# Seven products instead of eight for the last of the first MLP's second matmuls, and five smaller moves with it

## The chip, the cores and the metric

The kernel runs on one core of a Trainium2 chip. The metric is device time of one execution in microseconds (us). Engines are named as the profile names them: PE is TensorE's matrix multiply, PEld its weight load, DVE is VectorE, ACT is ScalarE, SP is the SyncE queue on which the DMA transfers are issued.

## What is computed

Linear attention with a decay for each head, and then two MLPs, one behind the other, on 3072 tokens of width 512 with a hidden width of 2048, all in float32:

```
state = gamma * state + einsum('bhd,bhe->bhde', k[t], v[t])
y[t]  = scale * einsum('bhd,bhde->bhe', q[t], state)
x = y.reshape(3072, 512)
h = x @ w_in;   g = h / (1 + exp(-1.702 * h));              x = g @ w_out
h = x @ w_in2;  g = max(h, 0) + alpha * min(h, 0);  out = g @ w_out2
```

The weights arrive as 64-bit words and are turned into float32 on the chip. An fp32 product is made of three: each operand is split into a high part that the fast matmul format holds exactly and a low rest (names ending in hi/lo, gh/gl, wh/wl, th/tl), and hi*hi, lo*hi and hi*lo are summed in PSUM.

## The kernel before

The tokens are six blocks of 512; each layer is worked off block by block. The program has three stretches.

**The plain part.** `steps` is a list of 32 steps (LEAD = 5 of block 0, all 16 of block 1, the other 11 of block 0). A step is one 128-wide slice of the hidden width: `mlp_h` (L531) makes 12 matmuls of 512 columns, the gate follows on ACT, `g_split` (L523) makes gh on ACT (L525) and gl on DVE (L526), and one step later `mlp_y` (L547) makes 12 matmuls into four PSUM banks (L558). Between the steps stand jobs, in numbered half-step slots: attention of a chunk of 128 tokens (`att_scores`, `att_out`, `att_x`), the conversion of weights, their stores to DRAM, and the sums of W_in slices (`conv_sums`, `conv_split`, slots in SUMS_IN). `base` is slot 64, the end of the plain part.

**The streamed pairs.** The other blocks of layer 1 and all of layer 2 come in five pairs (PAIRS, idx 0 to 4) of two token blocks. Their x @ w_in is made by seven products of 2 x 2 blocks instead of eight (the Strassen-Winograd scheme): a unit (`h_unit`) is one of the seven products for a quarter of a slice pair, 6 matmuls of 512 columns (L660) with one 256 KB weight piece `hw`, loaded in a ring that runs 6 units ahead. Eight quads of seven units make a pair. The partial results are joined on ACT (copies, L672) and DVE (adds, L675). Chunks 16 to 23 of the attention lie between the first 30 units or so.

The second matmul, g @ w_out, follows 36 units behind (YLAG). For idx 1 to 4 it has seven products too (`strassen_y`): a chunk is 6 matmuls (L758) with one 256 KB piece `yw`; it wants differences t1 to t4 of the gated blocks (L702), a split of each, and joins of the results (`y_out`, L771 on DVE, L781 on ACT). **For idx 0 it does not** (IDX_S = 1): it is made as in the plain part, by 12 matmuls a slice (`mlp_y`, in halves of 6), with hi and lo of W_out loaded again from DRAM (`woh`, `wol`, L644). In the second half of that, `slice_sums` and `conv_split` make the four sums of each W_out slice pair and store them (`wcout<-wb`), which idx 1 then uses.

**What sets the order.** Each engine runs its instructions in a fixed order. A framework makes that order from the order of the code, priorities (`tc.high_priority`) and its own estimates. The tiles live in 82 slots of SBUF (`take`, `give`), used again in the order in which they came free; a tile whose slot still has a store in flight must wait for that store. `give_stored` holds a slot back until `let_go` frees it a little later; the result tiles y of `mlp_out` and `y_out` use `give` at once. Loads of q, k, v and of the weight words go through a ring of five tiles (`issue`, `done`), in one order; the first chunks' q, k, v go through slots instead (`load_early`). SP's queue holds loads and stores in one order.

## Time and profile before

| | |
|---|---|
| three runs | 1059.97, 1061.17, 1063.59 us; median 1061.17 us |
| the profiled execution | 1063.32 us, its span 1061.5 us |
| PE busy, instructions | 1039.7 us (98%), 5980 |
| DVE busy, instructions | 847.8 us (80%), 1602 |
| ACT busy, instructions | 652.5 us (61%), 1344 |
| DMA | 292.07 MB, mean 275 GB/s |
| chain that ended last | PE 84%, DMA 7%, DVE 5%, ACT 3% |

The span is the time between the first and the last instruction; some 1.8 us of the execution lie around it. A matmul's record is longer than its share of the time, since the next begins before it has ended, so a busy PE need not be a PE at its peak. The windows view gives the busy time by stretches; in time, the plain part ends near 250 us, units alone run to 327 us, units and second matmuls by turns to 1006 us.

### The profile page before, as it was taken

The page shows a single profiled execution, that of the slowest core. Times are in us where ns is not written, and L with a number is a line of the kernel's source. Part 1 is how long each engine was busy: PE and PEld are TensorE (multiplying, and loading weights), DVE is VectorE, ACT ScalarE, POOL GpSimd, SP SyncE. Part 2 cuts the span into 40 slices and gives each one's busy share as a digit, 9 for nine tenths or more (in the row PEclk, how much of TensorE's full clock was granted, in tenths as well). Part 3 has the DMA queues.
Part 4 walks back from the last instruction along what each step waited for, and adds up shares of the span by engine and source line. Part 5 has one row for each costly group of instructions (what it writes and reads, how often), then busy time and mean ns, then how long its engine had stood idle before and what let it go on. Part 6 is the DMA issues. An engine that isn't in the chain of part 4 may idle for free.

```text
span 1061.5 us, 17729 instructions
## 1 busy us (share of the span) xinstructions
PE 1039.7 (98%) x5980; PEld 850.5 (80%) x5980; DVE 847.8 (80%) x1602; ACT 652.5 (61%) x1344; POOL 0.2 (0%) x4
## 2 busy tenths in 40 slices
PE   8999999999999999999999999989999999999998
PEld 5678877788878888888888878868888888888886
DVE  6999945584669877898899999999687897677792
ACT  6787744455566765556786586776555765546740
POOL 0000000000000000000000000000000000000000
PEclk9999999999999999999999999999999999999999
DMA  8679969779789999999999899978777775776571
GB/s 300 224 251 364 333 225 361 231 281 350 261 295 351 362 325 312 358 316 307 329 317 333 274 306 346 305 259 263 248 226 239 220 225 168 222 253 211 165 215 67
DMA packets 154139, 292.07 MB, mean 275 GB/s; under 512 B 16448, under 2 KB 33216, under 8 KB 154048
## 3 DMA queue, kind: packets, MB, share of 16 engines
q1 hardware_dynamic: 153760, 290.66, 81.1%
q8 instruction: 48, 0.79, 0.3%
q14 instruction: 43, 0.35, 0.1%
q10 hardware_dynamic: 288, 0.27, 0.1%
HBM read 214.32 MB, written 76.55 MB: 274 GB/s over the span
## 4 chain that ended last, share of the span: by engine, by line
PE 84%; DMA 7%; DVE 5%; ACT 3%; issue 1%; SPq 0%; DVEq 0%; ACTq 0%
PE py L758 26%; PE pa L660 18%; PE py L559 15%; PE pd L660 13%; PE ph L538 7%; DMA ld<-kv 2%; DMA wcin<-wb 2%; PE px L362 2%; PE sc L334 1%; DMA ld<-w 1%; DVE gl L526 1%; DVE a L345 1%; ACT v L327 1%; DMA early<-qk 1%; PE pu L362 0%
## 5 line engine op out<-in xcount | busy, mean ns | idle before, releaser
L660 PE MATMUL pa<-xo,hw 128*128 128x512 f32 x960 | 242.8, 390 | 1.9 <-ACT gw L517 1.6
L758 PE MATMUL py<-gh,yw 128*128 128x512 f32 x896 | 240.2, 389 | 1.0 <-DMA yw<-wcout 1.0
L660 PEld LDWEIGHTS pa<-xo,hw 128*128 128x128 f32 x960 | 179.7, 188 | 40.5 <-ACT gw L517 2.4
L758 PEld LDWEIGHTS py<-gh,yw 128*128 128x128 f32 x896 | 168.0, 188 | 36.8 <-DMA yw<-wcout 1.4
L660 PE MATMUL pd<-xo,hw 128*128 128x512 f32 x720 | 182.7, 390 | 0.0
L526 DVE TENSOR_TENSOR gl<-gw,gh 128x512 fp32r<-128x512 f32 x224 | 149.9, 685 | 38.9 <-ACT gh L525 34.5
L525 ACT CAST gh<-gw 128x512 fp32r<-128x512 f32 x224 | 135.8, 619 | 69.8 <-PE py L758 18.4
L660 PEld LDWEIGHTS pd<-xo,hw 128*128 128x128 f32 x720 | 134.8, 188 | 28.3
L758 PE MATMUL py<-gl,yw 128*128 128x512 f32 x448 | 138.2, 389 | 3.0 <-DVE gl L526 3.0
L758 PEld LDWEIGHTS py<-gl,yw 128*128 128x128 f32 x448 | 84.0, 188 | 20.7 <-DVE gl L526 3.4
L518 DVE SCALAR_TENSOR_TENSOR gw<-t,nalpha,gw 128x512 f32<-128x512 f32 x96 | 71.4, 746 | 18.6 <-ACT gw L517 18.3
L516 ACT ACTIVATE t<-gw 128x512 f32<-128x512 f32 x72 | 45.5, 632 | 49.9 <-DVE gw L675 49.3
L771 DVE TENSOR_TENSOR yc<-py,yc 128x512 f32<-128x512 f32 x79 | 50.7, 682 | 21.9 <-PE py L758 21.9
L212 ACT CAST wb<-s 128x256 fp32r<-128x256 f32 x128 | 48.0, 405 | 31.8 <-DVE s L279 16.5
L672 ACT COPY gw<-pa 128x512 f32<-128x512 f32 x80 | 46.5, 584 | 33.3 <-PE pa L660 32.4
L327 ACT ACTIVATE v<-ld,cst 128x64 f32<-128x64 f32 x168 | 44.5, 336 | 34.9 <-DMA ld<-kv 34.1
L675 DVE TENSOR_TENSOR gw<-pd,gw 128x512 f32<-128x512 f32 x80 | 54.6, 684 | 10.5 <-PE pd L660 10.5
L216 DVE TENSOR_TENSOR wb<-s,wb 128x256 fp32r<-128x256 f32 x128 | 50.2, 418 | 9.1 <-ACT wb L212 8.6
L538 PE MATMUL ph<-xhi,whi 128*128 128x512 f32 x128 | 52.3, 409 | 1.8 <-ACT xhi L420 1.1
L559 PE MATMUL py<-gh,whi 128*128 128x512 f32 x128 | 51.1, 399 | 0.7 <-ACT gh L525 0.7
L538 PE MATMUL ph<-xhi,wlo 128*128 128x512 f32 x128 | 51.3, 401 | 0.2 <-DVE wlo L242 0.2
L181 ACT ACTIVATE cvt<-ld 128x512 f32<-128x512 f32 x64 | 42.9, 673 | 12.4 <-DMA ld<-w 10.5
(100 smaller groups left out, 1616.7 us busy)
## 6 DMA issues: line engine op xcount, KB each, us to landing
hw<-wcin SPq DMA_DIRECT2D x280, 256.0 KB, 4.6
yw<-wcout SPq DMA_DIRECT2D x200, 256.0 KB, 3.8
ld<-w SPq DMA_DIRECT2D x64, 512.0 KB, 5.4
wcin<-wb SPq DMA_DIRECT2D x88, 256.0 KB, 4.8
wcout<-wb SPq DMA_DIRECT2D x88, 256.0 KB, 3.9
ld<-qk SPq DMA_DIRECT2D x21, 512.0 KB, 5.0
ld<-kv SPq DMA_DIRECT2D x21, 512.0 KB, 5.3
xl<-xsd SPq DMA_DIRECT2D x32, 256.0 KB, 5.3
```

Of the source, the lines that this page charges most:

```text
L212: nc.scalar.copy(out=w[:, 0:256], in_=src)
L216: nc.vector.tensor_tensor(out=w[:, 256:], in0=src, in1=w[:, 0:256].bitcast(F32), op=ALU.subtract)
L327: nc.scalar.activation(out=v[:, h, :], in_=vt[:, h * D:(h + 1) * D], func=AF.Copy, scale=decay_v[:, h:h + 1])
L518: nc.vector.scalar_tensor_tensor(out=g, in0=t, scalar=nalpha[:, ft:ft + 1], in1=g, op0=ALU.mult, op1=ALU.add)
L525: nc.scalar.copy(out=gh, in_=g)
L526: nc.vector.tensor_tensor(out=gl, in0=g, in1=gh.bitcast(F32), op=ALU.subtract)
L538: nc.tensor.matmul(out=ph, lhsT=w[:, k * P:(k + 1) * P], rhs=x[:, k, :], start=(n == 0), stop=(n == len(prods) - 1),)
L559: nc.tensor.matmul(out=py[e], lhsT=w, rhs=g, start=(begin and seen[e] == 1), stop=(end and seen[e] == 3))
L660: nc.tensor.matmul(out=ps, lhsT=w[:, 256 * part_ + k * P:256 * part_ + (k + 1) * P], rhs=x[2 * k + low], start=(n in (0, 1, 3) and m == 0) ...
L675: nc.vector.tensor_tensor(out=g, in0=ps, in1=g, op=ALU.add)
L758: nc.tensor.matmul(out=ps[e], lhsT=w[:, at:at + P], rhs=t, start=(fresh and seen[e] == 1), stop=(m == GQ - 1 and seen[e] == 3), skip_group ...
L771: add_ = lambda o, x: nc.vector.tensor_tensor(out=o, in0=ps, in1=x, op=ALU.add)
```

## The change

For idx 0 the second matmul becomes `strassen_y` as for the other pairs. The sums of the W_out slices are needed earlier for that and move into the plain part: slices 4 to 7 at slots 47 to 58, from hi and lo that are still on the chip, and slices 0 to 3 at slots 60 to 69, whose hi and lo are loaded again (`slice_load`). idx 0 therefore takes its slices in the order 4 to 7, 0 to 3, and the W_in sums are turned round in the same way. The q, k, v of chunks 16 to 23 come through slots, 2.5 slots ahead of their use. The products of v with the decay (L327) lose their priority. The differences t1 to t4 are each made a product earlier than they are used, where all of them stood with t2. The first six `yw` are loaded 12 units ahead, and result tiles y go through `give_stored`.

```diff
-IDX_S = 1
-QORD = [tuple(range(8)) if i != 1 else tuple(range(7, -1, -1)) for i in range(5)]
-WSTEPS = 6
-SUMS_IN = (37, 41, 45, 49, 53, 56, 59, 62)
+QORD = [(4, 5, 6, 7, 0, 1, 2, 3)] + [tuple(range(8))] * 4
+SUMS_IN = (53, 56, 59, 62, 37, 41, 45, 49)
+SUMS_OUT = (60, 63, 66, 69, 47, 51, 55, 58)
+LOADED = 4
...
+    def slice_load(i):
+        for f in (2 * i, 2 * i + 1):
+            assert ("out", 1, f) in stored
+            kept[f] = take("woh", dtype=F32R), take("wol", dtype=F32R)
+            for n in range(2):
+                nc.sync.dma_start(out=kept[f][n].bitcast(F32), in_=wo[f][n])
+
     def slice_sums(i):
         for f in (2 * i, 2 * i + 1):
+            ws = kept.pop(f, None)
+            hi, lo = ws or (w_hi["out", 1, f], w_lo["out", 1, f])
             raw["out", 1, f] = t = take("wsum")
-            hi, lo = wring[f]
...
-        with tc.high_priority(HG):
-            for h in range(H):
-                nc.scalar.activation(
...
+        for h in range(H):
+            nc.scalar.activation(
...
-            nc.sync.dma_start(out=dst, in_=y)
-            give(y)
-
-        return leave
+        nc.sync.dma_start(out=dst, in_=y)
+        give_stored(y)
...
             if which == "t2":
-                t2 = take("t2")
-                sub(g_of[b11], g_of[b12], g_of[b11])
-                sub(t2, g_of[b22], g_of[b11])
+                t2 = xt.pop(("y", b11))
+                ysplit[c] = g_split(t2, True)
                 sub(g_of[b21], g_of[b21], t2)
-                ysplit[c] = g_split(t2)
+                give(t2)
                 return
...
+            if which == "b11":
+                sub(g_of[b11], g_of[b12], g_of[b11])
+            if which == "b21":
+                t2 = xt["y", b11] = take("t2")
+                sub(t2, g_of[b22], g_of[b11])
+            if which == "t1":
+                sub(g_of[b12], g_of[b22], g_of[b12])
...
-        job(s_scores, att_scores, c, load=(("qk", c), ("kv", c)))
+        if c < 4 * per:
+            job(s_scores, att_scores, c, load=(("qk", c), ("kv", c)))
+        else:
+            job(s_scores - 2.5, load_early, c)
+            job(s_scores, att_scores, c)
...
+    for i in range(NQ):
+        if i < LOADED:
+            job(SUMS_OUT[i] - 2, slice_load, i)
+        job(SUMS_OUT[i], slice_sums, i)
+        job(SUMS_OUT[i] + 1, conv_split, "out", 1, i)
...
-    old = 4 * NF * IDX_S
     for u in range(len(units)):
         h_unit(u)
         past = u + 1 - YLAG
+        if past == -2 * YRING:
+            for c in range(YRING):
+                load_y(c)
         if past > 0:
-            y_turn(min(8 * past // NU, old) + max(0, past - old * NU // 8))
+            y_turn(past)
```

Three places show how the instructions move. The first is SP's queue near the end of the plain part, between the load of the sixth and of the seventh weight piece of the units (`hw`; `wcin` and `wcout` are the stored weights, `wb` a sum's two halves, `xl` the x of pair 0, `part` and `xsd` results). Before, its last rows:

```order
L249 DMA wcin_6_94<-wb 128x512
L644 DMA wol<-wo_121 128x512
L249 DMA wcin_7_95<-wb 128x512 x4
L644 DMA woh<-wo_122 128x512
L644 DMA wol<-wo_122 128x512
L644 DMA woh<-wo_123 128x512
...
L644 DMA wol<-wo_125 128x512
L608 DMA hw<-wcin_0_88 128x512
```

and now:

```order
L249 DMA wcout_0_104<-wb 128x512 x4
L294 DMA woh<-wo_122 128x512
L294 DMA wol<-wo_122 128x512
L597 DMA xsd_85<-y 128x512
L151 DMA ld<-w 128x1024
L597 DMA xsd_85<-y 128x512 x2
L151 DMA ld<-w 128x1024
L597 DMA xsd_85<-y 128x512
...
L169 DMA early<-kv 128x512 x2
L249 DMA wcin_3_91<-wb 128x512 x4
L613 DMA hw<-wcin_4_92 128x512
```

Stores of W_out sums, q, k, v of later chunks and words of layer 2's weights now stand ahead of the seventh piece. Counted in units of 256 KB, 65 transfers stood between the sixth and the seventh piece and 101 do now; up to the 21st piece it was 93 and is 147.

The second place is ACT's queue around steps 21 and 22, where block 1's results leave (`y`) and chunks 12 and 13 of the attention are worked on. Before:

```order
L513 ACTIVATE g<-ph 128x512
L525 CAST gh<-g 128x512
L327 ACTIVATE v<-ld,cst 128x64 x8
L581 COPY y<-py_1069 128x512
L581 COPY y<-py_1071 128x512
L212 CAST wb<-s_2334 128x256
L513 ACTIVATE g<-ph 128x512
L525 CAST gh<-g 128x512
L212 CAST wb<-s_2334 128x256
L327 ACTIVATE v<-ld,cst 128x64 x8
```

and now:

```order
L524 ACTIVATE g<-ph 128x512
L536 CAST gh<-g 128x512
L590 COPY y<-py_1069 128x512
L590 COPY y<-py_1071 128x512
L338 ACTIVATE v<-ld,cst 128x64 x16
L212 CAST wb<-s_2334 128x256 x2
L212 CAST wb<-s_2335 128x256
L524 ACTIVATE g<-ph 128x512
L536 CAST gh<-g 128x512
```

The eight products of v that chunk 12 needs stood behind the second gate (they are the later x8; chunk 13's stood first), and now stand ahead of it. The tiles g, gh, gl of that second gate and v of chunk 12 took the slots of the four y before; now they take others.

The third place is DVE's queue behind the last split of the plain part (`gl<-g,gh`), where the units begin (L675, now L666, joins their results; `a` is attention's mask). Before:

```order
L526 TENSOR_TENSOR gl<-g,gh 128x512
L470 TENSOR_TENSOR xo<-t_2824,xo 128x512
L575 TENSOR_TENSOR y<-py_2282,ld 128x512
...
L575 TENSOR_TENSOR y<-py_2285,ld 128x512
L675 TENSOR_TENSOR gw<-pd,gw 128x512 x2
L345 TENSOR_TENSOR a_3141<-sc_3131,cst 128x512
L345 TENSOR_TENSOR a_3143<-sc_3132,cst 128x512
L399 TENSOR_TENSOR t<-px,diag 128x256
```

and now:

```order
L584 TENSOR_TENSOR y<-py_2285,ld 128x512
L301 TENSOR_TENSOR wsum<-woh,wol 128x512
L279 TENSOR_TENSOR s_3201<-wsum 128x256
L216 TENSOR_TENSOR wb<-s_3201,wb 128x256
L666 TENSOR_TENSOR gw<-pd,gw 128x512 x2
L356 TENSOR_TENSOR a_3297<-sc_3287,cst 128x512
L356 TENSOR_TENSOR a_3299<-sc_3288,cst 128x512
L301 TENSOR_TENSOR wsum<-woh,wol 128x512
L279 TENSOR_TENSOR s_3200<-wsum 128x256
```

Sums of W_out slices stand between now, and the first of them waits for `woh` and `wol` from DRAM.

## Rows read from the trace of the kernel before

**Rows 1.** The chain that ended last, in order of time: start, length (us), what.

```profile
326.72 1.36 PE pa L660 x6
328.08 1.36 PE py L559 x6
...
1006.94 50.33 PE py L758 x222
```

**Rows 2.** Groups by line, whole run: busy us, mean ns | idle before.

```profile
L559 PE MATMUL py<-gh,woh 128*128 128x512 f32 x128 | 49.8, 389 | 0.0
```

**Rows 3.** Windows: length; busy us (count) of PE PEld DVE ACT POOL; clock, DMA share, GB/s.

```profile
60.00:140.00 80.00, 79.55 (x372) 65.50 (x363) 73.40 (x142) 59.89 (x117) 0.00 (x0) 1.00 0.95 329
...
325.00:405.00 80.00, 80.00 (x355) 66.26 (x354) 65.60 (x135) 50.74 (x105) 0.00 (x0) 1.00 0.97 347
405.00:490.00 85.00, 85.00 (x377) 70.41 (x376) 72.53 (x156) 48.35 (x102) 0.00 (x0) 1.00 0.97 331
...
540.00:600.00 60.00, 60.00 (x266) 49.73 (x265) 59.44 (x116) 44.37 (x90) 0.00 (x0) 1.00 0.92 305
600.00:660.00 60.00, 58.37 (x258) 48.00 (x257) 56.28 (x110) 40.26 (x81) 0.00 (x0) 1.00 0.93 321
660.00:720.00 60.00, 56.07 (x244) 45.30 (x243) 58.05 (x104) 46.37 (x92) 0.00 (x0) 1.00 0.87 292
```

**Rows 4.** Timeline of ACT, 172 to 184 us: start, length, what, [idle before].

```profile
179.49 0.60 ACT L513 ACTIVATE g<-ph 128x512 f32<-128x512 f32 x1 [4.34 <-DMA xsd<-y]
...
181.81 2.01 ACT L327 ACTIVATE v<-ld,cst 128x64 f32<-128x64 f32 x8
```

**Rows 5.** Timeline of PE, 181 to 183 us.

```profile
182.21 0.99 PE L362 MATMUL px<-v,ld 128*64 128x64 f32 x7 [1.64 <-ACT v L327]
```

**Rows 6.** Windows, columns as in rows 3.

```profile
183.40:190.20 6.80, 6.80 (x49) 5.26 (x48) 1.85 (x5) 1.03 (x4) 0.00 (x0) 0.50 0.83 278
```

**Rows 7.** Windows for the DMA rate, columns as in rows 3.

```profile
160.00:180.00 20.00, 20.00 (x209) 15.87 (x207) 10.95 (x24) 7.98 (x23) 0.00 (x0) 1.00 1.01 358
170.00:180.00 10.00, 10.00 (x97) 7.92 (x96) 5.72 (x13) 3.89 (x12) 0.00 (x0) 1.00 1.06 388
...
200.00:262.00 62.00, 62.00 (x438) 50.74 (x440) 40.39 (x82) 32.56 (x77) 0.00 (x0) 1.00 0.87 303
```

**Rows 8.** Timeline of SP's queue, 242 to 265 us.

```profile
243.18 6.65 SPq L608 DMA_DIRECT2D hw<-wcin  x9
...
263.35 1.62 SPq L608 DMA_DIRECT2D hw<-wcin  x3
```

**Rows 9.** The tile hw, 240 to 262 us: landing of its loads.

```profile
DMA to landing us min/median/max: 4.0/5.3/6.6
```

**Rows 10.** Timeline of PE: seventh unit, 21st unit.

```profile
259.70 1.07 PE L660 MATMUL pd<-xo,hw 128*128 128x512 f32 x4
...
290.75 1.52 PE L660 MATMUL pd<-xo,hw 128*128 128x512 f32 x6
```

**Rows 11.** Timeline of DVE, 690 to 707 us.

```profile
691.09 0.68 DVE L470 TENSOR_TENSOR xo<-t,xo 128x512 fp32r<-128x512 f32 x1
691.69 0.68 DVE L526 TENSOR_TENSOR gl<-gw,gh 128x512 fp32r<-128x512 f32 x1
...
693.56 0.74 DVE L518 SCALAR_TENSOR_TENSOR gw<-t,nalpha,gw 128x512 f32<-128x512 f32 x1
694.22 0.75 DVE L216 TENSOR_TENSOR wb<-s,wb 128x256 fp32r<-128x256 f32 x2
694.89 0.41 DVE L188 TENSOR_SCALAR cvt<-cvt 128x512 f32<-128x512 f32 x1
```

**Rows 12.** Timeline of PE, 690 to 712 us.

```profile
700.06 0.74 PE L758 MATMUL py<-gl,yw 128*128 128x512 f32 x2 [2.97 <-DVE gl L526]
...
706.07 0.50 PE L758 MATMUL py<-gh,yw 128*128 128x512 f32 x1 [0.96 <-DMA yw<-wcout]
```

**Rows 13.** Waits, 600 to 725 us: who for whom, us, times, longest.

```profile
PE pa L660 <- ACT gw L517: 1.6, 1, 1.6
```

More of the change, by code (lines that the diff above doesn't have):

```diff
@@ L545, in mlp_h, with mlp_y @@
             g_of[1, j, ft] = g_split(g)
-    def mlp_y(layer, j, ft, begin, end, carry, w, es=range(NP)):
-        if begin and es[0] == 0:
+    def mlp_y(layer, j, ft, begin, end, carry, w):
+        if begin:
             for e in range(NP):
@@ L553, in mlp_y @@
         cols = lambda w, e: w[:, e * P:(e + 1) * P]
-        prods = [(e, cols(w, e), gh) for e in es for w in (wh, wl)]
-        prods += [(e, cols(wh, e), gl) for e in es]
+        prods = [(e, cols(w, e), gh) for e in range(NP) for w in (wh, wl)]
+        prods += [(e, cols(wh, e), gl) for e in range(NP)]
         seen = [0] * NP
@@ L564, in mlp_y @@
             with tc.high_priority(HP):
-                leave = mlp_out(layer, j, e, carry)
-            leave()
-        if es[-1] == NP - 1:
-            del g_of[layer, j, ft]
-            give(gh, gl)
+                mlp_out(layer, j, e, carry)
+        del g_of[layer, j, ft]
+        give(gh, gl)
     def mlp_out(layer, j, e, carry):
@@ L619, in load_y @@
     def load_y(c):
-        if c < len(ychunks) and ychunks[c][0] == "s":
-            idx, grp, p, m = ychunks[c][1:]
+        if c < len(ychunks):
+            idx, grp, p, m = ychunks[c]
             load_piece(yw, "yw", "out", PAIRS[idx][0], QORD[idx][GQ * grp + m], p)
-    ysteps = [(idx, t, f if t == 0 else NF - 1 - f) for idx in range(IDX_S) for t in range(2) for f in range(NF)]
-    wkey = [f for _, _, f in ysteps]
-    wring = {}
-    ychunks = [("o", n, half) for n in range(len(ysteps)) for half in range(2)]
-    ychunks += [
-        ("s", idx, grp, p, m)
-        for idx in range(IDX_S, len(PAIRS))
+    ychunks = [
+        (idx, grp, p, m)
+        for idx in range(len(PAIRS))
         for grp in range(NQ // GQ)
@@ L634, in tile_linear_attention_two_mlps @@
     ]
-    def load_wo(n):
-        for f in wkey[n:n + 2 * WSTEPS]:
-            if f in wring:
-                continue
-            if len(wring) == WSTEPS or ("out", 1, f) not in stored:
-                return
-            wring[f] = take("woh", dtype=F32R), take("wol", dtype=F32R)
-            for t, src in zip(wring[f], (0, 1)):
-                nc.sync.dma_start(out=t.bitcast(F32), in_=wo[f][src])
     chain = {}
@@ L691, in y_split @@
         with tc.high_priority(HG):
-            if ychunks[c][0] == "o":
-                _, n, half = ychunks[c]
-                if half == 0:
-                    idx, t, f = ysteps[n]
-                    g_of[1, 2 * PAIRS[idx][1] + t, f] = g_split(g_of.pop((idx, t, f)))
-                return
-            _, idx, grp, p, m = ychunks[c]
+            idx, grp, p, m = ychunks[c]
             f = 2 * QORD[idx][GQ * grp + m]
@@ L722, in y_chunk @@
     def y_chunk(c):
-        if ychunks[c][0] == "o":
-            _, n, half = ychunks[c]
-            idx, t, f = ysteps[n]
-            first, end = n % NF == 0, n % NF == NF - 1
-            if idx == IDX_S - 1 and t == 1:
-                if half == 0 and f % 2:
-                    slice_sums(f // 2)
-                elif f % 2 == 0 and half == 0:
-                    conv_split("out", 1, f // 2)
-            mlp_y(1, 2 * PAIRS[idx][1] + t, f, first, end, None, wring[f], range(2 * half, 2 * half + 2))
-            if half:
-                if f not in wkey[n + 1:n + 2 * WSTEPS]:
-                    give(*wring.pop(f))
-                load_wo(n + 1)
-        else:
-            strassen_y(c)
-        load_y(c + YRING)
-    def strassen_y(c):
-        _, idx, grp, p, m = ychunks[c]
+        idx, grp, p, m = ychunks[c]
         w, (th, tl) = yw.popleft(), ysplit.pop(c)
@@ L768, in strassen_y @@
                     leave()
+        load_y(c + YRING)
     def y_out(idx, grp, p, e, ps, final):
@@ L948, in tile_linear_attention_two_mlps @@
                 load_h(u)
-    load_wo(0)
     for s, step in queue:
```

12 lines of the change are left out of this document (6 added, 6 removed).

## The prediction

> **What bounds the kernel now.** I read the chain that ended last first. From 327 us on it is PE's matmuls with nothing between them, groups of six in 1.36 us, by turns from the units and from the second matmul [rows 1]. At the end 222 matmuls take 50.33 us, which is 0.2267 us for one. A record is longer (389 ns in the groups by line [rows 2]), because records overlap; so I count matmuls by 0.2267 us and not by their records. Then the windows: in the two stretches from 325 to 490 us, where pair idx 0 has its second matmul, PE is busy without a gap, DVE 82% and 85% of the time [rows 3]. So fewer matmuls there make the kernel shorter, unless another engine or the DMA takes over. Third come PE's few waits; the timelines show the largest near 182 us [rows 5] and near 700 us [rows 12].
>
> **The matmuls taken away.** For idx 0 the second matmul had three groups of 128 on `woh` and `wol` (gh on each, gl on `woh`; the first is in [rows 2]), 384 together. Now it has 2 groups of slices x 7 products x 4 = 56 chunks of 6, 336. 48 x 0.2267 = **-10.9 us**. They stood in a stretch without a gap, so all of it is on the path.
>
> **The waits that y caused.** Near 175 us ACT waits 4.34 us before a gate, for the store of block 1's results [rows 4]: the gate's tile took the slot of a y whose store was in flight. Behind it in ACT's queue stood the products of v for chunk 12, which begin at 181.81. PE waits for them 1.64 us [rows 5]. Right behind that wait, from 183.4 to 190.2 us, PE's granted clock is 0.50, its level of 1.2 GHz [rows 6], where it is 1.00 (2.4 GHz) before and after [rows 7]. Half of 6.8 us is 3.4 us. The order of the changed kernel puts these products ahead of the gate, and the gate in another slot. If both go, **-5.0 us**; the bounds are 0 (another tile waits there) and -5.0. I take -5.0, since two parts of the change remove the same chain.
>
> **The end of the plain part: more DMA.** The sums of W_out cost stores and loads that stood between 325 and 490 us, where DMA was 97% busy, and now stand ahead of 300 us; so do earlier q, k, v and words of layer 2. Up to the issue of the seventh `hw`, 36 more transfers of 256 KB stand in SP's queue (101 for 65), and up to the 21st 54 more (147 for 93). One takes 0.262 MB / 358 GB/s = 0.73 us at the rate of the busiest 20 us [rows 7]. From 200 to 262 us the DMA moved 303 GB/s, so 62 us x 55 GB/s = 3.4 MB, 13 transfers, fit in for nothing. Of the 54, 41 are left, 30 us; the 21st unit starts at 290.75 [rows 10], its piece was issued by 264.97 at the latest [rows 8] and landing took up to 6.6 us [rows 9], so it had some 20 us to spare. That leaves a wait of 10 us. For the seventh piece: issued at 243.18, landed by 249.8, used at 259.70, 10 us to spare; 23 x 0.73 = 17 us, a wait of 7. Waits of one queue are not added; the largest counts. At the rate of 325 to 405 us, 347 GB/s [rows 3], a transfer takes 0.755 us, ten fit in, and the 21st waits 13 us. At 388 GB/s, the best ten microseconds [rows 7], 0.675 us each, 20 fit in, and it waits 3 us. Less is possible: PE's order now has up to two chunks of attention more ahead of the seventh unit, and waits for late k and v there become shorter. So the bounds are 0 and 13; I take **+5.0 us**, between the two rates and a little below the middle, because part of the wait takes in small waits that PE has there anyway.
>
> The Trainium skill (Perfetto Trace Analysis, section Engine Utilization) says that 358 GB/s is a core's share of memory when both cores of a pair draw on it, and that a core alone can reach about 120% of it. By that, 430 GB/s by estimate, the wait would be nothing and the sum 5 us lower. The best rows here stop at 388 GB/s, 108%; no stretch of this trace shows more.
>
> **DVE at the same place.** From step 24 to the end of the plain part DVE's queue now holds 43 operations of 512 columns and 87 of 256, where it held 35 and 50. They follow each other by 0.60 and 0.335 us [rows 11]: 55 us, 38 before. PE's part is 8 steps of 24 matmuls, 43.5 us, and some 6.5 us of attention. DVE thus falls 5 us behind. A split is wanted one step after its gate, some 5 us later, so this costs about nothing by itself; in 60 to 140 us, too, DVE was 92% busy beside a full PE [rows 3]. Without that slack it would be up to 5 us, but at the same time as the DMA wait, so I add nothing.
>
> **The pair's second matmul.** It gains 32 differences, 24 splits and 16 joins on DVE, 72 x 0.60 = 43 us, and loses the sums, 16 of 512 and 64 of 256 columns, 31 us. In the 28 units and 28 chunks where it is densest, 97 operations of 512 and 48 of 256 columns make 74.5 us against 56 x 1.36 = 76.2 us of PE: 98%. Between 540 and 600 us DVE was 99% busy and PE lost nothing; from 600 to 720 it was 94% and 97% busy and PE lost 5.6 us [rows 3]. So the bounds are 0 and about 6; the first is nearer, since a `gl` has three chunks' time ahead of its use (AHEAD): **+0.5 us**. The casts on ACT rise by 24, but ACT is busy 63% and 57% there. The W_out pieces of 1 KB runs rise from 24 to 48 and take the place of hi and lo; bytes in that stretch fall.
>
> **The waits from 600 to 720 us.** They are 2.97 us for a `gl` [rows 12], 0.96 us for a `yw` [rows 12] and 1.6 us for a gate's read of PSUM [rows 13]. DVE's queue was unevenly filled: counted as above from its order, in the last 28 groups of six before some 705 us it held 41.2 us of work for 38.1 us of PE, in the 28 before only 34.0. Now these are 38.2 and 38.2, and the differences no longer stand three in a row ahead of a split. But in the 140 groups up to there DVE now has 218 operations of 512, 95 of 256 columns and 40 scaled ones at 0.66 us [rows 11], 189 us for 190.4 of PE. The bounds are -5.5 and +3; I take **-2.0 us**.
>
> The late q, k, v, the earlier first `yw` and the reversed order of slices I cost at nothing apart from this: their transfers are counted above, and at 327 us `yw` has 12 units to land.
>
> **Sum.** -10.9 - 5.0 + 5.0 + 0.5 - 2.0 = -12.4 us. The profiled execution took 1063.3 us, so 1050.9; it lies 2.1 us above the median of the runs shown, so I predict **1049 us** for the median.
>
> **Rivals.**
> - *The DMA keeps up.* If it holds its best rate, or PE's new order of attention covers the rest, the +5.0 goes: 1044 us. For it: the stretch at 388; against it: it lasted ten microseconds, and 358 over twenty is the next. Chance 0.22.
> - *DVE binds in the pair's second matmul.* At 98% it loses what 600 to 720 us lost, 5.6 us, in place of 0.5: 1054 us. Against it stands the stretch at 99% without a loss. Chance 0.15.
> - *The chain near 182 us stays*, with another tile in the slot of a y, or the clock falls at another place: 1054 us. The change would then not do there what it says. Chance 0.10.
> - *The queue of transfers takes all back.* If stores from SBUF and loads of weights together get no more than the 303 GB/s of 200 to 262 us, nothing fits in free; 54 x 0.865 = 46.7 us less 20 to spare is a wait of 26 us instead of 5: 1070 us, slower. It decides from a rate of about 318 GB/s down, where the wait passes 21 us. Against it stand 329 to 347 GB/s over 80 us [rows 3]. Such a wait among small matmuls could also bring the lower clock again. Chance 0.05.
>
> **How the numbers follow.** The forecast has 0.48, with a range of its own from 1045 to 1053. A measurement of this kernel tells about 0.3% from no change, 3.2 us: faster means below 1058.0, slower above 1064.4. Forecast and first rival lie wholly below; of the two at 1054, some 0.19 of 0.25. That makes 0.89 faster, 0.06 same, 0.05 slower. The range is 1040 to 1058: below, the DMA rival with most of the waits from 600 to 720 us gone as well; above, one of the two at 1054 with 4 us more of DMA wait.
>
> **What would show it.** 5932 matmuls instead of 5980, all groups of the second matmul of idx 0 on `yw`. No wait of ACT for `xsd<-y` near 175 us, and a clock of 1.00 from 140 to 250 us. In the stretch from 245 to 300 us PE idle by about 5 us, for `hw` or early k and v or a `wsum` that waits for `woh`, with DMA at 97% or more from 205 us. From 320 to 480 us PE without gaps and DVE near 97%. Waits of 3 to 4 us from 600 to 720 us. I am wrong if PE waits more than 10 us before 300 us, if the clock falls there, or if the pair's second matmul shows gaps.

## The result, and the profile after

The changed kernel takes **1066.43 us** (median of 11 runs, 1063.79 to 1070.52), the kernel before, on the same chip, 1061.17 us (11 runs, 1058.80 to 1065.75). The ratio is 1.0052, 95% interval 1.0038 to 1.0066: 5 us slower, where 12 us faster was forecast, and outside the range. The profiled execution took 1067.40 us, its span 1065.6 us.

Where the time went shows best between fixed points of PE's work: the first matmuls of steps and of units (times between starts, us, counted from the two traces).

| stretch | before | after | difference | prediction's term |
|---|---|---|---|---|
| start to step 18 | 137.4 | 136.2 | -1.2 | none |
| step 18 to step 24 | 59.5 | 55.3 | -4.2 | -5.0 (waits that y caused) |
| step 24 to first unit | 53.3 | 58.4 | +5.1 | 0 (DVE at the same place) |
| first to 43rd unit | 92.6 | 106.8 | +14.2 | +5.0 (more DMA) |
| 43rd to 113th unit | 201.4 | 191.2 | -10.2 | -10.9, +0.5 |
| 113th to 201st unit | 246.3 | 247.3 | +1.0 | -2.0 |
| 201st unit to the last matmul | 266.7 | 266.7 | 0.0 | 0 |

All eight groups of six matmuls that were saved lie in the fifth row. The fourth row holds the same matmuls in both kernels (48 groups of six and 592 small ones of the attention), so its 14.2 us are lost time. I call that row the seam. Over it, the windows of the kernel before and of the changed kernel are (columns as in rows 3):

```profile
250.20:342.90 92.70, 90.62 (x882) 74.16 (x881) 62.99 (x147) 53.99 (x136) 0.00 (x0) 1.00 0.88 307
```

```profile
249.90:356.70 106.80, 100.15 (x881) 80.34 (x880) 82.53 (x191) 63.06 (x153) 0.00 (x0) 0.95 0.96 348
```

PE's idle time grew from 2.08 to 6.65 us, which is 4.6 us, and the lower clock of 266 to 276 us (below) cost 5.1 us. The other 4.5 us lie where PE counts as busy at its full clock, among the attention's small matmuls, which now stand in another order between the units; no row puts them down to a wait, and no run here separates them. The clock part is that of one execution, at a mean granted clock of 0.993. Over the eleven runs the mean is 0.9955, and the kernel before has 0.9954 to 0.9968 in its runs beside the experiments. One thousandth of the span is 1.07 us, so in the run times the clock accounts for some 1.4 of the 5 us at most.

Windows of the changed kernel by stretches:

```profile
245.50:249.00 3.50, 3.50 (x9) 2.76 (x10) 2.81 (x7) 2.66 (x10) 0.00 (x0) 0.51 0.51 191
250.00:300.00 50.00, 44.97 (x431) 36.36 (x430) 32.63 (x76) 27.29 (x73) 0.00 (x0) 0.90 1.00 355
266.00:276.20 10.20, 10.17 (x98) 8.80 (x99) 5.12 (x12) 3.38 (x10) 0.00 (x0) 0.50 1.05 392
...
330.00:405.00 75.00, 74.50 (x355) 61.09 (x354) 72.14 (x142) 54.59 (x109) 0.00 (x0) 1.00 0.87 308
405.00:480.00 75.00, 74.44 (x329) 61.38 (x328) 64.72 (x122) 45.59 (x86) 0.00 (x0) 1.00 0.89 308
...
600.00:660.00 60.00, 59.05 (x257) 47.62 (x256) 56.03 (x109) 40.22 (x77) 0.00 (x0) 1.00 0.93 318
660.00:720.00 60.00, 56.63 (x245) 44.98 (x244) 57.92 (x108) 45.48 (x90) 0.00 (x0) 1.00 0.88 292
```

From 330 to 480 us PE is nearly full and DMA has more air than in [rows 3]: the seven products do there what they should. From 250 to 300 us PE is busy 45 of 50 us at a mean clock of 0.90. The half clock that stood at 183 us [rows 6] is gone from there; it now stands at 245.5 to 249 us and at 266 to 276.2 us.

The timeline of PE has the waits that answer to [rows 5] and [rows 10] (last bracket: idle before, and who ended it):

```profile
162.72 0.69 PE L373 MATMUL px<-v,ld 128*64 128x64 f32 x16 [1.81 <-ACT wb L212]
...
245.47 0.76 PE L570 MATMUL py<-gh,whi 128*128 128x512 f32 x1 [2.53 <-ACT gh L536]
...
262.43 1.16 PE L345 MATMUL sc<-early 64*128 64x128 f32 x16 [0.95 <-DMA early<-qk]
266.03 0.34 PE L373 MATMUL px<-a,v 128*64 128x64 f32 x1 [2.43 <-DVE a L356]
```

None of them is a wait for `hw`, by which the prediction had counted; no wait of PE over 0.25 us from 200 to 400 us is one for it. For the unit loads the tile view of `hw` from 262 to 340 us has

```profile
DMA to landing us min/median/max: 3.6/5.7/6.9
```

close to [rows 9]. The piece of the seventh unit had landed 4.2 us before its use, that of the 21st 7.3 us. What was late stands in SP's queue (timeline of SP; `woh` and `wol`, the high and low parts of W_out, are called the halves from here on):

```profile
244.24 0.67 SPq L294 DMA_DIRECT2D wol<-wo  x1
250.15 0.32 SPq L597 DMA_DIRECT2D xsd<-y  x1
...
253.69 0.66 SPq L294 DMA_DIRECT2D woh<-wo  x1
254.39 0.50 SPq L294 DMA_DIRECT2D wol<-wo  x1
254.99 0.92 SPq L169 DMA_DIRECT2D early<-qk  x2
```

and in the waits of SP from 236 to 262 us:

```profile
SPq L597 <- DVE y L584: 5.2, 1, 5.2
```

SP issues nothing for 5.2 us. It waits to store block 0's result y, which DVE makes when PE has ended the plain part. Behind that store stand the halves of the next W_out slice and the q, k of the second late chunk. The halves land at 260.95 us (issue at 254.39, 6.56 us to landing), and DVE, which had reached their sum, stood until then (timeline of DVE):

```profile
261.05 0.69 DVE L301 TENSOR_TENSOR wsum<-woh,wol 128x512 f32<-128x512 f32 x1 [3.11 <-DMA wol<-wo]
...
265.19 1.28 DVE L356 TENSOR_TENSOR a<-sc,cst 128x512 f32<-128x512 f32 x2
```

Behind that sum on DVE, 4.1 us from its start, stand the masks `a` for which PE waits 2.43 us. Right after this wait the granted clock is 0.50 for 10.2 us, half of which is 5.1 us. This chain is read from the trace: each link shows its wait, but no run moves the store alone.

The wait at 245.47 us has another cause (timeline of ACT):

```profile
242.12 0.74 ACT L212 CAST wb<-s 128x256 fp32r<-128x256 f32 x2 [0.93 <-DVE s L279]
242.76 1.13 ACT L480 CAST xo<-xl 128x512 fp32r<-128x512 f32 x2
243.80 0.59 ACT L524 ACTIVATE g<-ph 128x512 f32<-128x512 f32 x1
...
244.80 0.62 ACT L536 CAST gh<-g 128x512 fp32r<-128x512 f32 x1
```

A cast of the sums waits on ACT for DVE, which is behind with those sums; the gate of the last step stands behind the cast. In the table this and the clock of 0.51 after it are the greater part of +5.1 us.

### The profile page after: what moved, and what is told of

It is laid out like the page before. It is cut to its first block, busy times and chain, and to the rows that moved or that the text cites. A ratio compares the mean times of both kernels' runs of the same rounds, so it can differ in the third digit from the quotient of the medians.

```text
span 1065.6 us, 17820 instructions
## 1 busy us (share of the span) xinstructions
PE 1039.2 (98%) x5932; PEld 845.8 (79%) x5932; DVE 889.9 (84%) x1674; ACT 674.6 (63%) x1372; POOL 0.2 (0%) x4
## 4 chain that ended last, share of the span: by engine, by line
PE 73%; DVE 11%; DMA 10%; ACT 3%; issue 1%; SPq 1%; DVEq 0%; ACTq 0%
PE py L728 31%; PE pa L651 16%; PE pd L651 12%; PE py L570 5%; PE ph L549 5%; DMA hw<-wcin 2%; PE px L373 2%; DVE gl L537 2%; DMA early<-kv 2%; DMA wol<-wo 2%; DMA ld<-kv 1%; PE sc L345 1%; DVE gw L529 1%; DVE s L279 1%; DVE wb L216 1%
## 5 line engine op out<-in xcount | busy, mean ns | idle before, releaser
L728 PE MATMUL py<-gh,yw 128*128 128x512 f32 x1120 | 300.4, 390 | 1.4 <-DMA yw<-wcout 0.9
L728 PEld LDWEIGHTS py<-gh,yw 128*128 128x128 f32 x1120 | 209.8, 188 | 46.3 <-ACT gh L536 1.4
L536 ACT CAST gh<-gw 128x512 fp32r<-128x512 f32 x240 | 145.9, 621 | 75.6 <-PE py L728 23.9
L537 DVE TENSOR_TENSOR gl<-gw,gh 128x512 fp32r<-128x512 f32 x240 | 161.8, 688 | 37.7 <-ACT gh L536 29.1
L728 PE MATMUL py<-gl,yw 128*128 128x512 f32 x560 | 173.1, 390 | 1.7 <-DVE gl L537 1.7
L728 PEld LDWEIGHTS py<-gl,yw 128*128 128x128 f32 x560 | 104.8, 188 | 24.9 <-DVE gl L537 3.3
L742 DVE TENSOR_TENSOR yc<-py,yc 128x512 f32<-128x512 f32 x99 | 63.7, 685 | 26.7 <-PE py L728 26.7
L663 ACT COPY gw<-pa 128x512 f32<-128x512 f32 x80 | 46.9, 586 | 40.7 <-PE pa L651 37.6
L666 DVE TENSOR_TENSOR gw<-pd,gw 128x512 f32<-128x512 f32 x80 | 54.9, 687 | 8.0 <-PE pd L651 7.9
L687 DVE TENSOR_TENSOR gw<-gw 128x512 f32<-128x512 f32 x80 | 54.7, 687 | 0.4
L570 PE MATMUL py<-gh,wlo 128*128 128x512 f32 x128 | 51.0, 399 | 0.0
```

Source lines behind the costliest of these rows:

```text
L536: nc.scalar.copy(out=gh, in_=g)
L537: nc.vector.tensor_tensor(out=gl, in0=g, in1=gh.bitcast(F32), op=ALU.subtract)
L570: nc.tensor.matmul(out=py[e], lhsT=w, rhs=g, start=(begin and seen[e] == 1), stop=(end and seen[e] == 3))
L666: nc.vector.tensor_tensor(out=g, in0=ps, in1=g, op=ALU.add)
L687: sub = lambda o, x, y: nc.vector.tensor_tensor(out=o, in0=x, in1=y, op=ALU.subtract)
L728: nc.tensor.matmul(out=ps[e], lhsT=w[:, at:at + P], rhs=t, start=(fresh and seen[e] == 1), stop=(m == GQ - 1 and seen[e] == 3), skip_group ...
```

## The experiments

Fifteen kernels were run. The 24 chunks of the program are numbered 0 to 23; where the texts on record say "chunks 16 to 31", read 16 to 23. Stretches below are as in the table: "seam" is from the first to the 43rd unit, 92.6 us before and 106.8 after. Each kernel ran beside the kernel before on one chip, not beside the changed kernel, so "less" and "back" against the changed kernel are differences of the two ratios, unless medians are named. The ratios' intervals are 1.5 to 3.5 us wide to either side; differences of 2 or 3 us are not clear of that. Stretches and waits are those of one profiled execution each.

**1. y's slots alone.** In the kernel before, `mlp_out`:

```diff
             nc.sync.dma_start(out=dst, in_=y)
-            give(y)
+            give_stored(y)
```

> The kernel before with one part of the change alone: the slots of y in the plain part become free two steps after their store is issued, not at once. My prediction's term 'the waits that y caused': ACT's wait of 4.34 us for the store of a y, PE's wait at 182 us and the stretch of clock 0.50 behind it go, 4 to 5 us less, 1056 to 1057 us, ratio 0.995 to 0.997. Rival 'another wait takes its place': the chunk's chain of v, mask and product is late there for another reason; less than 2 us, 1059 to 1062 us, ratio 0.998 to 1.001.

Measured: 1062.31 us, ratio 1.0016 (0.9994 to 1.0038). The chain went: the clock is 1.00 from 183 to 191 us,

```profile
183.00:191.00 8.00, 8.00 (x119) 6.32 (x115) 2.98 (x6) 3.24 (x10) 0.00 (x0) 1.00 0.76 273
```

but PE has a new wait of about its size 20 us earlier, where ACT makes v for another chunk late:

```profile
161.71 0.69 PE L362 MATMUL px<-v,ld 128*64 128x64 f32 x16 [1.84 <-ACT wb L212]
```

Step 18 to 24 is 3.6 us shorter in the profile, the 113th to 201st unit 2.9 us longer (with a half clock of 3.4 us that the kernel before did not have there), and the median shows no gain. The rival comes nearer. What took the 3.6 us back is not shown: each profile is one execution.

**2. Four slices' sums later.**

```diff
-SUMS_OUT = (60, 63, 66, 69, 47, 51, 55, 58)
+SUMS_OUT = (70, 71, 72, 73, 47, 51, 55, 58)
```

> The sums of W_out slices 0 to 3 are made in slots 70 to 73 (units 24 to 34, from about 316 us on) and their halves loaded two slots ahead; before they stood in slots 60 to 69 (about 235 to 310 us). Theory 'crowded seam' (the 16 loads, 16 stores and the work on DVE of these sums push masks, early q, k, v and PE's attention back between 240 and 340 us, where the changed kernel lost 18.7 us against the kernel before): 10 to 14 us come back, 1053 to 1057 us, ratio to the kernel before 0.992 to 0.996, and no stretch of clock 0.50 from 266 to 276 us. Rival 'late q, k, v': the late loads into slots are to blame, and this moves less than 3 us, 1063 to 1067 us, ratio 1.002 to 1.006. Rival 'only moved': the work does the same harm from 316 us on, 1064 to 1068 us, with the lost time of PE between 316 and 350 us.

Measured: 1069.08 us, ratio 1.0071 (1.0046 to 1.0096). This lies above the ranges of all three. The wait at 245 us is gone, and the first to the 21st unit takes 44.7 us where the changed kernel took 59.9; but the seam as a whole is still 101.8 us, and the 43rd to 113th unit takes 197.1 us for 191.2. The loss has moved, as the third theory has it: from 316 to 345 us DVE is 96% busy and PE 78%, and from 312 to 400 us SP waits for DVE's pieces before it can store them (window; waits of SP):

```profile
316.00:345.00 29.00, 22.68 (x128) 17.38 (x123) 27.87 (x64) 18.03 (x41) 0.00 (x0) 1.00 0.94 320
```

```profile
SPq L249 <- DVE wb L216: 8.4, 8, 3.2
```

**3. Sums not computed.** `slice_stored` stores the loaded halves in the sums' places.

```diff
+        if i < LOADED:
+            job(SUMS_OUT[i] + 1, slice_stored, i)
+            continue
         job(SUMS_OUT[i], slice_sums, i)
```

> Left out: the sums of W_out slices 0 to 3. Their 16 loads and 16 stores stay where they are, but what is stored are the loaded halves, so DVE has 40 operations less and ACT 16 casts less there. Theory 'DVE's queue' (a sum that waits for its load holds the mask behind it, and DVE has more work than PE leaves time for from step 24 on): 9 to 13 us come back, 1053 to 1057 us, ratio 0.992 to 0.996, attention from 250 to 300 us near that of the kernel before. Rival 'transfers' (the bytes in DMA's queue are to blame, whoever uses them): less than 3 us, 1063 to 1068 us, ratio 1.002 to 1.006.

Measured: 1061.21 us, ratio 1.0004 (0.9987 to 1.0020), 5 us less than the changed kernel, between the two theories. The windows of the changed kernel and of this one:

```profile
238.00:250.00 12.00, 9.47 (x35) 7.36 (x34) 10.88 (x26) 8.30 (x23) 0.00 (x0) 0.86 0.77 274
```

```profile
238.00:250.00 12.00, 12.00 (x55) 9.94 (x54) 9.47 (x19) 8.70 (x22) 0.00 (x0) 1.00 1.00 333
```

With DVE's work for these sums away, the wait at 245 us and its half clock are gone (last step to first unit 8.2 us for 12.6). The seam keeps 102.7 us, without any half clock in it: q, k of chunk 17 are still issued behind block 0's stores and PE waits 1.0 us for them. Its waits add up to 5.3 us; what the rest of the seam's excess is, no row says.

**4. Sums not loaded.** The sums are made from a constant.

```diff
-            kept[f] = take("woh", dtype=F32R), take("wol", dtype=F32R)
-            for n in range(2):
-                nc.sync.dma_start(out=kept[f][n].bitcast(F32), in_=wo[f][n])
+            kept[f] = ()
```

> Left out: the 16 loads of 256 KB of the W_out halves for slices 0 to 3; the sums are made with the same operations from a constant, and stored as before. Theory 'transfers': 16 x 0.72 us = 11.5 us of DMA time leave the stretch; 8 to 12 us come back, 1054 to 1058 us, ratio 0.993 to 0.997. Rival 'DVE's queue': the sum no longer waits 3.1 us for its load, but the work on DVE stays; 2 to 5 us come back, 1061 to 1064 us, ratio 1.000 to 1.003. Rival 'late q, k, v': less than 2 us.

Measured: 1052.37 us, ratio 0.9916 (0.9884 to 0.9949), 14 us less than the changed kernel. The seam is 94.2 us. By their bytes, 16 loads at 0.73 us are 11.7 us, which lies within the interval (11 to 18 us), so this run shows that the loss hangs on these loads, but not whether on their bytes, their slots or their place in the queue. Experiment 8 keeps the bytes.

**5. Halves loaded earlier.**

```diff
-            job(SUMS_OUT[i] - 2, slice_load, i)
+            job(SUMS_OUT[i] - 5, slice_load, i)
```

> The halves of slices 0 to 3 are loaded five slots ahead of their sums instead of two (about 13 to 24 us instead of 5 to 10); bytes, operations and the sums' places stay. Theory 'a sum at the head of DVE's queue' (a sum that waits for its load holds mask a of chunk 16 behind it, 2.6 us of PE, and brings the lower clock from 266 to 276 us, 5 us): 5 to 8 us come back, 1058 to 1061 us, ratio 0.997 to 1.000. Theory 'bytes' (the queue of transfers as a whole is what PE waits for): the wait moves to another transfer, less than 3 us, 1063 to 1068 us, ratio 1.002 to 1.006.

Measured: 1063.66 us, ratio 1.0013 (0.9993 to 1.0032), 4 us less. The program issued the halves around block 0's store in part all the same (wol at 253.74, SP standing 4.7 us before), and now q, k of chunk 17 came late: 2.17 us of PE. What stands behind SP's wait changed, not the wait. The 4 us lie between the two theories.

**6. Late q, k, v by the ring.**

```diff
-        if c < 4 * per:
-            job(s_scores, att_scores, c, load=(("qk", c), ("kv", c)))
-        else:
-            job(s_scores - 2.5, load_early, c)
-            job(s_scores, att_scores, c)
+        job(s_scores, att_scores, c, load=(("qk", c), ("kv", c)))
```

> One part of the change undone: q, k, v of chunks 16 to 31 come by the ring of five tiles again, in the order of use, and not into slots two and a half steps ahead. Theory 'late q, k, v' (the loads into slots stand behind others in SP's queue and land late, chunk 17's keys 1.2 us after PE wants them; two chunks' attention stands ahead of the seventh unit): 4 to 10 us come back, 1056 to 1062 us, ratio 0.995 to 1.001. Theory 'crowded seam' by the sums: within 3 us of the changed kernel, or some us slower since the ring's tiles are held by words of layer 2: 1063 to 1070 us, ratio 1.002 to 1.009.

Measured: 1063.58 us, ratio 1.0028 (1.0013 to 1.0044), 2.5 us less, hardly clear of noise and less than the theory asked for. The seam is 103.7 us; what it gains up to the 21st unit (42.7 for 59.9) it mostly loses after it (61.0 for 46.9).

**7. v first.**

```diff
-        for h in range(H):
-            nc.scalar.activation(
+        with tc.high_priority(HG):
+            for h in range(H):
+                nc.scalar.activation(
```

> The changed kernel with one part undone: the products of v have their high priority again. The trace of the changed kernel has PE waiting 1.98 and 0.53 us at 162.7 and 180.6 us where ACT makes v after the casts of the sums. Theory 'v behind casts': these go, 2 to 4 us less, 1062 to 1064 us, ratio 1.001 to 1.003. Rival 'v ahead holds the gates' (what the change was to avoid: v waits for its load with the gate behind it): same or slower, 1066 to 1070 us, ratio 1.004 to 1.009.

Measured: 1064.18 us, ratio 1.0030 (1.0010 to 1.0051), 2.3 us less, the theory's size but not clear of noise, and in the profile step 18 to 24 is 1.7 us longer. Small, and not the cause.

**8. The same loads issued by POOL.**

```diff
-                nc.sync.dma_start(out=kept[f][n].bitcast(F32), in_=wo[f][n])
+                nc.gpsimd.dma_start(out=kept[f][n].bitcast(F32), in_=wo[f][n])
```

> The changed kernel with the 16 loads of the W_out halves issued by POOL, which does nothing else, in place of SP; bytes and operations are the same. Theory 'order in SP's queue' (SP issues in order and waits for slots, so loads of early q, k, v and of the sums hold each other up): the sums' loads no longer stand between others, 5 to 12 us come back, 1055 to 1062 us, ratio 0.994 to 1.000. Rival 'bytes at the seam': the same transfers share the same DMA engines; within 3 us of the changed kernel, 1063 to 1069 us, ratio 1.002 to 1.008.

Measured: 1058.90 us, ratio 0.9965 (0.9950 to 0.9980): **9 us back with the same bytes**, and faster than the kernel before. The seam is 95.7 us. SP has issued q, k, v of chunk 17 and q, k of chunk 18 before it comes to the store, for which it now waits 1.6 us; the sum finds its halves there; and DMA moves 392 and 385 GB/s where the changed kernel moved 355 (SP's timeline, DVE's, windows):

```profile
242.37 1.23 SPq L169 DMA_DIRECT2D early<-qk  x2
243.69 0.97 SPq L169 DMA_DIRECT2D early<-kv  x2
245.18 1.40 SPq L169 DMA_DIRECT2D early<-qk  x2
...
249.01 0.33 SPq L597 DMA_DIRECT2D xsd<-y  x1
```

```profile
260.66 0.68 DVE L301 TENSOR_TENSOR wsum<-woh,wol 128x512 f32<-128x512 f32 x1
```

```profile
250.00:275.00 25.00, 20.57 (x219) 16.44 (x218) 17.39 (x42) 14.88 (x44) 2.16 (x4) 1.00 1.04 392
275.00:300.00 25.00, 25.00 (x290) 20.29 (x291) 19.23 (x46) 18.61 (x52) 0.00 (x0) 1.00 1.04 385
```

The wait at 245 us, DVE's, is still there (12.8 us from the last step to the first unit). And now PE does wait for `hw`: 2.33 us at the seventh unit, as it does for 1.54 us in experiment 12. The wait that the prediction had counted comes to light when the larger one is gone. The edit also let the framework order the engines anew: chunk 17's products with v now stand behind the seventh unit. So the 9 us are for queue and order together; the clock, a mean of 0.997 over the ten runs, is under 2 of them. That a second queue moves more is not needed to explain the rate: in experiment 12 SP alone issues the loads and DMA moves 387 GB/s over 50 us.

**9. Late loads ahead of the store, all on SP.**

```diff
-            job(s_scores - 2.5, load_early, c)
+            job(s_scores - 5.5, load_early, c)
```

> The changed kernel with the loads of late q, k, v placed five and a half slots ahead of their use in place of two and a half. In SP's order three chunks' loads then stand ahead of the stores of block 0's results; in the changed kernel SP waited 5.2 us for the first of these (245 to 250 us), with chunk 17's q and k and the next halves of W_out behind it. Bytes and operations are the same, all issued by SP, and the sums' loads still stand on SP. Theory 'order in SP's queue': chunk 17's q and k are there in time and PE's waits at 262 and 266 us and the clock of 0.50 behind them go or shrink; 5 to 10 us come back, 1056 to 1061 us, ratio 0.995 to 1.000. Rival 'only POOL's second queue helps' (two queues get more through): within 3 us of the changed kernel, 1063 to 1068 us, ratio 1.002 to 1.007.

Measured: 1067.78 us, ratio 1.0067 (1.0036 to 1.0097): nothing back, the expectation missed, and the time lies in the rival's range. The trace says what came in place of the gain. SP stands still 6.4 us all the same, q, k, v are there in time, and now it is the halves that come late; two sums wait for them on DVE, with the masks behind, PE waits 6.54 us, and the clock is 0.50 from 264.4 to 278.1 us. Over the ten runs the mean clock is 0.990 for the changed kernel's 0.9955, some 5 us (timelines of SP, DVE and PE):

```profile
240.78 1.12 SPq L249 DMA_DIRECT2D wcin<-wb  x2
248.68 0.32 SPq L597 DMA_DIRECT2D xsd<-y  x1
...
261.09 0.32 SPq L294 DMA_DIRECT2D wol<-wo  x1
```

```profile
265.23 0.69 DVE L301 TENSOR_TENSOR wsum<-woh,wol 128x512 f32<-128x512 f32 x1 [2.04 <-DMA wol<-wo]
...
267.22 0.69 DVE L301 TENSOR_TENSOR wsum<-woh,wol 128x512 f32<-128x512 f32 x1 [0.84 <-DMA wol<-wo]
```

```profile
270.93 0.37 PE L373 MATMUL px<-a,v 128*64 128x64 f32 x1 [6.54 <-DVE a L356]
```

Experiments 5 and 9 together, as their traces have it: whichever loads stand behind the store are late, and the halves are the worse ones, since a sum that waits for them holds DVE. That is a reading of two traces; neither run gave back what its theory asked for.

**10. Words kept.** The converted words of the first five W_out blocks stay in a slot until their sums are made; nothing is loaded again.

```diff
-SUMS_OUT = (60, 63, 66, 69, 47, 51, 55, 58)
+SUMS_OUT = (36, 38, 41, 44, 47, 51, 55, 58)
...
-        if kind == "in":
+        if kind == "in" or ft < KEPT:
             raw[key] = t
```

> A version that could beat both: for the first five W_out blocks the converted words stay in a slot until the sums of slices 0 to 3 are made, in slots 36 to 44 (about 125 to 190 us, where DVE is busy 3 to 5 of 8 us and DMA 3% from 136 to 144 us), so none of these slices is loaded again. 16 loads of 256 KB and five operations of 512 columns on DVE less, and the sums of these slices away from the seam. Theory 'bytes': at least what leaving out the 16 loads gave (ratio 0.992), plus a part of what leaving out the sums' work gave; 1046 to 1053 us, ratio 0.986 to 0.993. Theory 'DVE's queue': the same sign, 1052 to 1058 us, ratio 0.992 to 0.997. Rival 'only moved': the stores and the work on DVE disturb the chunks' attention between 140 and 215 us, 1056 to 1064 us, ratio 0.996 to 1.003.

Measured: 1065.73 us, ratio 1.0064 (1.0040 to 1.0088), against every expectation. Its clock accounts for that: the mean over the ten runs is 0.988 for the kernel before's 0.996, some 8 us. The profiled execution is the slowest of the ten, 1073.64 us (windows, clock third from the end):

```profile
186.00:200.00 14.00, 11.47 (x62) 7.66 (x66) 6.83 (x15) 4.25 (x13) 0.00 (x0) 0.63 1.05 395
262.00:285.00 23.00, 19.98 (x173) 16.96 (x174) 9.84 (x24) 8.43 (x28) 0.00 (x0) 0.55 1.04 382
```

Each stretch begins with a wait among the chunks' small matmuls (2.56 us at 188.5, 3.82 us at 264.4 us).

The second wait bears on SP's order, for nothing is loaded again here. SP waits 4.9 us for block 0's y, the q, k of chunk 16 stand behind that store, and PE waits for them (timelines of SP and PE):

```profile
252.67 0.32 SPq L587 DMA_DIRECT2D xsd<-y  x1
...
256.10 1.02 SPq L169 DMA_DIRECT2D early<-qk  x2
```

```profile
264.42 0.98 PE L335 MATMUL sc<-early 64*128 64x128 f32 x5 [3.82 <-DMA early<-qk]
```

In experiment 11, with the same transfers on the same queue, SP waits for the store as long (5.3 us), but these loads stand ahead of it, and PE has no wait for them:

```profile
245.89 0.90 SPq L169 DMA_DIRECT2D early<-qk  x2
...
253.57 0.33 SPq L587 DMA_DIRECT2D xsd<-y  x1
```

From the first to the 21st unit it is 56.1 us here and 46.6 us there. DVE's sums have moved as well between the two, so this too is queue and order together, but no bytes and no second queue.

**11. Words kept, later slices spread.** Against 10:

```diff
-SUMS_OUT = (36, 38, 41, 44, 47, 51, 55, 58)
+SUMS_OUT = (36, 38, 41, 44, 47, 52, 58, 63)
```

> As words_kept, and the sums of slices 5 to 7 stand later, in slots 52, 58 and 63 in place of 51, 55 and 58, so DVE has two slices' sums less from 200 to 248 us, where it is busy without a gap in the changed kernel, and they stand beside the units. Theory 'DVE's queue' (PE's wait of 2.7 us at 245 us for a split and the clock of 0.50 behind it come from DVE's work in steps 24 to 31): 2 to 4 us less than words_kept. Theory 'bytes': within 1.5 us of words_kept.

Measured: 1060.63 us, ratio 0.9985 (0.9967 to 1.0002), 5 us less than words kept by the medians, 8 by the ratios (four of ten runs of words kept took over 1068 us); the mean clock, 0.9945 for 0.988, is the greater part of that. What is left is a sum on DVE that waits for a slot whose store is in flight, as the chain of waits shows, and a clock of 0.50 behind it:

```profile
181.84 4.31 DMA wcout<-wb
186.18 0.75 DVE s L279 x2
```

With the edit of 6 on top of this:

> As words_kept_spread, with q, k, v of chunks 16 to 31 by the ring of five tiles again. Theory 'late q, k, v' (their loads into slots and the two chunks ahead of the seventh unit are still what the seam loses, 26.6 us longer or shorter from the first unit to the 21st): 2 to 4 us less than words_kept_spread, as in the changed kernel, 1056 to 1059 us, ratio 0.995 to 0.998. Rival 'only with the sums there': with the 16 loads gone slots are as good as or better than the ring, whose tiles are held by words of layer 2; 0 to 6 us more, 1060 to 1067 us, ratio 0.999 to 1.006.

Measured: 1057.91 us, ratio 0.9968 (0.9953 to 0.9982), 1.8 us less by the ratios, not clear of noise; the theory is neither shown nor ruled out. With the edit of 7:

> As words_kept_spread, with the high priority of the products of v given back (this part of the change undone), so ACT makes v of a chunk ahead of casts. Theory 'v behind casts' (PE's waits among the chunks, 2.2 us at 190 us and others, come from v or from casts that stand ahead of it): 2 to 5 us less, 1055 to 1058 us, ratio 0.994 to 0.997. Rival 'masks on DVE decide': within 2 us, 1058 to 1062 us, ratio 0.997 to 1.001.

Measured: 1060.27 us, ratio 0.9994 (0.9975 to 1.0013): nothing, as the rival has it. That it is the masks which decide was not tested further.

**12. Words kept, sums earlier.** Against 11:

```diff
-SUMS_OUT = (36, 38, 41, 44, 47, 52, 58, 63)
+SUMS_OUT = (34, 36, 38, 44, 47, 52, 58, 63)
```

> As words_kept_spread, but the sums of slices 0, 1 and 2 stand in slots 34, 36 and 38 in place of 36, 38 and 41, so that their eight stores of a slice and their operations on DVE lie ahead of 165 us and two more slots are free from step 19 to 22. In words_kept_spread a sum on DVE waited at 186 us for the store of a tile whose slot it took, mask a behind it, PE 2.2 us, and then the clock was 0.50 from 192 to 199 us. Theory 'slots' (that wait comes from stores that hold the few free slots): the wait and the clock behind it go, 4 to 6 us less than words_kept_spread, 1054 to 1057 us, ratio 0.993 to 0.996. Rival 'the clock falls anyway' (at the next wait among the chunks' small matmuls): within 2 us of words_kept_spread, 1058 to 1062 us, ratio 0.997 to 1.001.

Measured: **1052.41 us, ratio 0.9916 (0.9883 to 0.9949)**, 7 us less than the version before it for three numbers (four runs). The wait for the store is gone from the profile, no stretch of half clock is left from 120 to 420 us, the seam is 94.4 us, and DMA moves 387 GB/s over 50 us:

```profile
250.00:300.00 50.00, 47.22 (x513) 38.08 (x512) 30.85 (x73) 31.20 (x85) 0.00 (x0) 1.00 1.05 387
```

**13. The same with the ring.**

> words_kept_early with q, k, v of chunks 16 to 31 by the ring of five tiles again. Theory 'late q, k, v cost by themselves' (words_kept_spread gained 2.7 us by the ring, the changed kernel 2.5): 2 to 4 us less than words_kept_early, 1048 to 1051 us, ratio 0.987 to 0.990. Rival 'only less of the lower clock in those pairs': words_kept_early already has clock 1.00 at the seam, so within 2 us of it, 1051 to 1055 us, ratio 0.990 to 0.994.

Measured: 1052.80 us, ratio 0.9906 (0.9881 to 0.9931). The rival holds: with the loads gone, slots and ring are alike (seam 94.4 both). These two versions are the fastest whole kernels here, 9 to 10 us below the kernel before; the one of experiment 8 beats both kernels too, by 4 us and 9.

## Why the prediction was wrong, point by point

- **The matmuls taken away, -10.9 us: right.** From the 43rd to the 113th unit stand 140 groups of six for 148 and take 191.2 us for 201.4; 140 x 1.36 = 190.4, so PE lost 0.8 us there, near the +0.5 taken for the pair's second matmul. DVE at 96% (72.14 of 75 us) did not bind.
- **The end of the plain part: more DMA, +5.0 us within 0 to 13: the step that failed.** Measured: +14.2 us, above the upper bound. The working counted bytes against a rate, and only for `hw`. The rate was misread to begin with: it says that no stretch of the trace shows more than 388 GB/s and takes 358 from "the busiest 20 us", but the kernel before moved 392 GB/s over another 20 us (its window):

```profile
335.80:355.80 20.00, 20.00 (x90) 16.54 (x89) 14.99 (x31) 13.07 (x26) 0.00 (x0) 1.00 1.05 392
```

  The same bytes go at 392 and 385 GB/s at the seam when they are issued in time (experiment 8), and `hw` was not what PE waited for there. What the trace shows in its place is SP's order: a store that cannot start before PE ends the plain part holds 5.2 us of issues, the halves behind it hold a sum on DVE, the sum holds the masks, PE waits, and the clock is 0.50 for 10.2 us. The prediction had named "a `wsum` that waits for `woh`" among its signs, and that a fall of the clock there would prove it wrong, but gave neither a price in the sum. Shown is that the 16 loads cost it, and not by their bytes: issued by POOL they give 9 us back (8), left out 14 (4). How the 9 us divide between the queue and the new order of the chunks is not shown, and 4.5 of the 14.2 us belong to no wait in these rows.
- **DVE at the same place, 0 us: wrong, +5.1.** The working found DVE 5 us behind, counted on the slack of the splits, and laid what might be left under the DMA wait. But the casts of the sums stand on ACT ahead of a gate, so the lag reached PE through ACT: 2.53 us, and 3.5 us of half clock (1.7 us). Without these sums' work both go (3, and 2 where it was moved away); that is shown.
- **The waits that y caused, -5.0 us: the chain was there and went, the gain does not show in the median.** Step 18 to 24 is 4.2 us shorter in the profile, but this part of the change alone gives a ratio of 1.0016 (0.9994 to 1.0038). ACT's late v at another chunk is one part of why; another is that 3.4 of the 5.0 us were the clock of one execution.
- **The waits from 600 to 720 us, -2.0 us: about half of it.** PE's idle time in these windows fell from 5.6 to 4.3 us. The row of the table is 1.0 us longer all the same; the other kernels with this second matmul, whose edits lie elsewhere, range from 246.8 to 251.8 us in that row, so the 1.0 tells nothing. The waits were put down to DVE's uneven work. The waits of the changed kernel from 590 to 725 us name stores as well, and those of the kernel before, from 600 to 725 us, did so more:

```profile
ACT t L527 <- DVE gw L666: 6.4, 7, 2.3
...
ACT gh L536 <- DMA wcin<-wb: 2.6, 2, 1.8
```

```profile
ACT gh L525 <- DMA wcin<-wb: 5.2, 2, 4.0
```

  A cast on ACT that waits for a slot whose store is in flight is not DVE's amount of work. No kernel here tested either; it stays open.
- The nearest rival was the queue of transfers that takes all back (1070 us, chance 0.05). Its size was near by luck: its mechanism, a rate under 318 GB/s, was not there. The changed kernel moved 355 GB/s from 250 to 300 us and was slower all the same. Its remark that a wait among small matmuls could bring the lower clock came true.

The Trainium skill (Perfetto Trace Analysis, section Engine Utilization) puts the practical ceiling of a lone core at about 120% of 358 GB/s. Here 50 us at 387 GB/s are 108%: above the rate that the prediction took, below the page's ceiling. By the page the DMA term would have been nothing. As to the rate that was the better reading, though the 1.5 to 2.3 us for `hw` in experiments 8 and 12 are not nothing.

## What to carry to other kernels

Count an added transfer by its place in the issuing queue before its bytes: ask which earlier entry of that queue must wait for compute, and what stands behind it. Then ask which engine meets the late tile first, and what stands behind that instruction: a sum that nobody needs soon, ahead of masks that PE needs now, turned a late load into PE's wait. Put optional work where its inputs are still on the chip, and then try its places: words kept on the chip took 1065.7, 1060.6 and 1052.4 us with the sums in different slots (10 to 12).
